# Chunked scan kernel: C sent compact and spread on chip, scores on row halves, loads and the first y reordered

## The chip, the cores and the metric

The kernel runs on one core of a Trainium2 chip. The metric is the device time of one execution in microseconds, the median of several runs; less is better.

## The reference

Three stages follow each other. The first is a chunked scan over 4 batches, 8 heads and 768 positions, head size 32, state size 16, chunks of 32 positions. The other two are a routed layer with 8 experts and a wide layer.

```python
for c in range(nc):                                    # 24 chunks
    cum = np.cumsum(la, axis=-1)
    L = np.exp(cum[..., :, None] - cum[..., None, :]) * causal
    M = np.einsum('bhin,bhjn->bhij', Cc, Bc) * L       # scores, masked
    y_intra = np.einsum('bhij,bhjd->bhid', M, xc)
    y_inter = np.einsum('bhin,bhnd->bhid', Cc, state) * np.exp(cum)[..., None]
    y[:, :, sl] = y_intra + y_inter
    state = decay_full * state + sum_j(Bc x xc * decay_from_j)
...
logits = x @ w_gate; e = argmax(logits); p = softmax(logits)[e]
out = p * (relu(x @ w1[e]) @ w2[e])
...
g = relu(x @ w_in) ** 2; return g @ w_out
```

## The kernel before, in words

The program is written out by hand for each engine: `manual_schedule` keeps the order in which the lines are called, and every engine, and every DMA queue, takes its instructions strictly in that order.

**Tiles and phases.** The scan (the function `attention`) works on 24 tiles of 128 tokens. Four tiles make a phase (a pair of batches, 256 positions), so there are six phases, 0 to 5; `ph, r = divmod(i, 4)` in the code. The loop `for i in range(-2, 24)` runs these steps, each a few tiles ahead of the next:

- `st_S` makes the scores. TensorE writes `sc` (C against B, L425), VectorE multiplies by the masked decay `Qm` into `M` (L428). It does so for tiles r = 0 and r = 1 of a phase, one batch each; r = 2 and 3 use the same `M`.
- `st_D` makes the state increments `dS` of two tiles on TensorE (L444), and `st_R` adds them on VectorE, 8 instructions a pair of tiles (L461). `dS` is one buffer for each batch, so the next `st_D` waits for the `st_R` before it.
- `st_Y` makes y on TensorE from `M` and X (L473) and from the state and C transposed, `CT` (L480). VectorE scales it into `row` (L485).
- `st_TT` transposes two tiles of rows on TensorE (`tp`, L502), and ScalarE copies them to `xt` (L505). `logits` (L511) and `logits2` (L518) turn four tiles of `xt` into gate logits.
- `gateA` picks the expert on VectorE; its first instruction is the maximum `mx` (L535). `gateB` counts ranks on TensorE (L557 to L561), VectorE makes slots from them (L566 to L571), and the queue stores the four rows to DRAM (`xs<-row`, L572). `spotA` makes one-hot tables, `lf` on VectorE (L581) and `lo` in five instructions on ScalarE (L591, L592). `spotB` multiplies them on TensorE (L602). `order` (L621 to L632) sorts the experts after phase 3.

The first `mx` of a phase's gate is a mark that comes four times in an even rhythm; the prediction measures stretches from mark to mark.

**Block layouts.** X for the increments and C for the scores lie in one tile `XC` ([128, 4, 2048], two buffers), each spread over four blocks with zeros between them: partition c, c+4, c+8, ... holds data only in block c. `blank_c` writes the zeros once (VectorE L315, ScalarE L312), and four loads a phase for X and four for C bring 32 partitions each (L290); in phases 0 to 2 some loads bring both halves. The C half is also doubled with zeros (`e`) on the host. So `sc` can be one matmul over 128 partitions for each head: 256 columns, 32 weight columns, four heads side by side in the four column strips of the array. `BB` holds B in two layouts (512 KB a phase, L284), `XA` is X for y, four loads a phase (L296), `CT` two loads (L300). `blank_x` zeroes XA, for the second buffer as two memsets on GpSimd (L662, L663).

**Queues.** All these loads go through SP's queue in the order of the calls. Eight semaphores are handed round among the DMAs, so a load waits until the eighth one before it has landed.

**The decay sums** `cum`, `cu2` borrow the score buffers (tag `sc`, two of one PSUM bank); `decay()` (L370, L371) writes into `cum` after the first increments.

After the scan come the routed layer (class `Moe`) and the wide layer (class `Mlp`), whose matmuls follow each other on TensorE.

## Time and profile before

| what | us |
|---|---|
| median of 3 runs | 511.07 (510.78 to 513.61) |
| the profiled execution's own time | 510.4 |
| its span, first to last instruction | 508.4 |
| TensorE busy | 491.3 (97%) |
| VectorE busy | 372.4 (73%) |
| ScalarE busy | 309.4 (61%) |
| GpSimd busy | 99.4 (20%) |
| bytes moved by DMA | 51.22 MB |

The profile gives one execution, with times from its first instruction. A row of the timeline says when a group of equal instructions started, how long it took in all, which line and tiles it has, and in brackets how long the engine had been idle before it and what ended that. TensorE's matmuls overlap, so the step from one start to the next tells more than the length of one. The scan fills roughly the first 80 us of the span.

### The profile page before, as it was taken

What the parts mean: (1) busy time and instruction counts of PE and PEld (TensorE: products, weight loads), DVE (VectorE), ACT (ScalarE), POOL (GpSimd) and SP (SyncE); (2) the same over time, 40 slices, a digit from 0 to 9 for tenths busy, and PEclk for the clock granted to TensorE, in tenths of its full rate; (3) what the DMA queues carried; (4) which work ended last, traced back from release to release, by engine and by line L of the source; (5) the groups of instructions that cost most, each with busy time, mean ns of one, the idle gap of its engine ahead of it and who ended that gap; (6) DMA issues with size and microseconds to landing.
All of it is one profiled execution on the core that took longest, in us unless ns stands there. A gap on an engine that the chain in (4) does not pass through costs nothing.

```text
span 508.4 us, 11650 instructions
## 1 busy us (share of the span) xinstructions
PE 491.3 (97%) x4537; PEld 459.1 (90%) x4537; DVE 372.4 (73%) x844; ACT 309.4 (61%) x636; POOL 99.4 (20%) x131
## 2 busy tenths in 40 slices
PE   7899798999999999999999999999999999999995
PEld 3677678899999999999999999899999999999995
DVE  8787688669898899994666767534888888676521
ACT  8332335376656666755986889776555555455684
POOL 6953210543331130000000000101500300031031
PEclk9999999999999999999999999999999999999999
DMA  8886866767676656530001100000100000010010
GB/s 258 271 254 219 276 196 209 227 163 191 188 222 169 176 193 191 183 84 2 2 1 43 43 0 1 12 10 12 74 2 0 23 23 1 1 43 1 1 43 24
DMA packets 20476, 51.22 MB, mean 101 GB/s; under 512 B 6561, under 2 KB 6690, under 8 KB 20418
## 3 DMA queue, kind: packets, MB, share of 16 engines
q1 hardware_dynamic: 17442, 43.04, 27.2%
q0 software_dynamic: 2832, 7.01, 5.1%
q8 instruction: 37, 0.61, 0.5%
q10 hardware_dynamic: 144, 0.40, 0.2%
q14 instruction: 21, 0.17, 0.1%
HBM read 44.06 MB, written 6.37 MB: 99 GB/s over the span
## 4 chain that ended last, share of the span: by engine, by line
PE 85%; issue 4%; ACT 3%; DVE 3%; DMA 2%; POOL 1%; SPq 1%; ACTq 0%; another core or an unknown queue 0%; POOLq 0%; DVEq 0%
PE u L1261 24%; PE o L953 14%; PE h L937 14%; PE h L1081 11%; PE h L1169 9%; PE u L1169 2%; DMA XC<-in_xc_dram 2%; PE dS L444 2%; PE y L473 2%; PE sc L425 2%; PE y L480 1%; PE tpm L918 1%; ACT XC L312 1%; PE tp L502 1%; DVE st L461 1%
## 5 line engine op out<-in xcount | busy, mean ns | idle before, releaser
L1261 PE MATMUL u<-wol,ga 128*128 128x256 f32 x384 | 108.0, 281 | 0.0
L1261 PE MATMUL u<-woh,ga 128*128 128x256 f32 x384 | 107.7, 281 | 0.0
L1261 PE MATMUL u<-woh,gb 128*128 128x256 f32 x384 | 107.7, 280 | 0.0
L1275 POOL DMA_INDIRECT out_dram<-ob,idx x24 | 26.6, 1109 | 278.9 <-ACT ob L1274 274.3
L1088 DVE TENSOR_TENSOR gb<-q,ga 128x256 fp32r<-128x256 f32 (+1 forms) x64 | 35.7, 558 | 57.5 <-ACT ga L1087 57.4
L1261 PEld LDWEIGHTS u<-woh,ga 128*128 128x128 f32 x384 | 72.3, 188 | 1.4
L1261 PEld LDWEIGHTS u<-wol,ga 128*128 128x128 f32 x384 | 72.3, 188 | 1.3
L1261 PEld LDWEIGHTS u<-woh,gb 128*128 128x128 f32 x384 | 72.5, 189 | 0.1
L940 ACT ACTIVATE hh<-h 128x256 fp32r<-128x256 f32 (+8 forms) x72 | 33.9, 472 | 52.6 <-PE h L937 49.0
L1081 PE MATMUL h<-zz,wih 128*128 128x512 f32 (+1 forms) x192 | 59.1, 356 | 0.0
L942 DVE SCALAR_TENSOR_TENSOR hl<-h,hh 128x256 fp32r<-128x256 f32 (+8 forms) x72 | 38.2, 530 | 16.9 <-ACT hh L940 16.8
L953 PE MATMUL o<-hl,whi 128*128 128x256 f32 (+8 forms) x144 | 47.6, 331 | 0.1
L953 PE MATMUL o<-hh,whi 128*128 128x256 f32 (+8 forms) x144 | 47.7, 331 | 0.0
L953 PE MATMUL o<-hh,wlo 128*128 128x256 f32 (+8 forms) x144 | 47.4, 329 | 0.2 <-DVE wlo L174 0.2
L937 PE MATMUL h<-xh,whi 128*128 128x208 f32 (+7 forms) x128 | 44.3, 346 | 0.2 <-DVE hl L942 0.2
L174 DVE TENSOR_TENSOR wlo<-wst,whi 128x512 fp32r<-128x512 f32 x64 | 43.2, 676 | 0.0
L937 PE MATMUL h<-xh,wlo 128*128 128x208 f32 (+7 forms) x128 | 42.9, 335 | 0.0
L937 PE MATMUL h<-xl,whi 128*128 128x208 f32 (+7 forms) x128 | 42.8, 335 | 0.0
L1085 ACT ACTIVATE q<-h 128x256 f32<-128x256 f32 (+1 forms) x64 | 30.9, 482 | 13.2 <-PE h L1081 11.3
L1081 PEld LDWEIGHTS h<-zz,wih 128*128 128x128 f32 x192 | 34.9, 188 | 4.3
L1169 PE MATMUL h<-zz,s 128*128 128x256 f32 x216 | 38.4, 286 | 0.0
L883 POOL DMA_INDIRECT xr<-xs,where x27 | 27.6, 1024 | 41.9 <-PE tpm L918 26.6
(250 smaller groups left out, 1191.6 us busy)
## 6 DMA issues: line engine op xcount, KB each, us to landing
wst<-in_wq_dram SPq DMA_DIRECT2D x32, 512.0 KB, 4.8
w<-in_win_dram SPq DMA_DIRECT2D x8, 512.0 KB, 6.5
w<-in_wout_dram SPq DMA_DIRECT2D x8, 512.0 KB, 4.3
XC<-in_xc_dram SPq DMA_DIRECT2D x28, 128.0 KB, 4.1
xs<-row SPq DMA_DIRECT2D x6, 516.0 KB, 4.0
BB<-in_bb_dram SPq DMA_DIRECT2D x6, 512.0 KB, 4.2
XA<-in_xa_dram SPq DMA_DIRECT2D x24, 128.0 KB, 3.8
XC<-in_xc_dram SPq DMA_DIRECT2D x10, 256.0 KB, 4.4
```

The lines of the kernel that those rows point to most:

```text
L174: eng.tensor_tensor(lo[:, w], st[:, w], hi[:, w].bitcast(F32), ALU.subtract)
L883: k.nc.gpsimd.indirect_dma_start(out=self.xr[key][:, j], out_offset=None, in_=rows, in_offset=bass.IndirectOffsetOnAxis(ap=at, axis=0))
L937: nc.tensor.matmul(ps, ring.up(wt, e, f, kd), xt[:, kd], start=(i == 0), stop=(i == 5))
L940: nc.scalar.activation(a, ps, ACTF.Relu)
L942: rest = lambda: nc.vector.scalar_tensor_tensor(b, ps, 0.0, a.bitcast(F32), ALU.max, ALU.subtract)
L953: nc.tensor.matmul(self.yps[e][d][:, c:c + n], ring.down(wt, e, f, d), ht, start=(f == 0 and i == 0), stop=(f == 7 and i == 2))
L1081: nc.tensor.matmul(ps, wt[:, kd, m * 128:m * 128 + 128], zt[t][:, kd], start=(i == 0), stop=(i == 5))
L1085: nc.scalar.activation(q, ps, ACTF.Relu)
L1088: nc.vector.tensor_tensor(b, q, a.bitcast(F32), ALU.subtract)
L1169: mm(o, w, z, start=start and i == 0, stop=True, skip_group_check=True)
L1261: nc.tensor.matmul(o, gt[:, q * 128:q * 128 + 128], wt[:, m], start=(m == first and i == 0 and h == 0), stop=(m == last and i == 2), skip_ ...
L1275: ins = nc.gpsimd.indirect_dma_start(out=k.out, out_offset=bass.IndirectOffsetOnAxis(ap=self.idx[:, c:c + 1], axis=0), in_=ob, in_offset=N ...
```

## The change

C is no longer sent with zeros. `bs` holds B and C side by side ([128, 1024], one load a phase, `load_s`), and the other layout of B is a load of its own (`bc`, 256 KB, `load_b`). Both have two buffers. `XC` shrinks to X alone ([128, 4, 1024]), and its four loads bring 128 KB each; the four loads of C are gone.

`expand(ph)` makes the spread C on chip, into `CB` (two buffers): four instructions of 128x512, each C times a column of zeros and ones (`C_POS`). For phase 0 VectorE does it, for the others ScalarE, in the loop at i = -1, 3, 7, 11 and 15, a phase ahead of its scores.

The scores of both batches of a phase are made at once at r = 0, into one `sc` of two banks. Each head is two matmuls instead of one, over partitions 0 to 63 and 64 to 127, of 128 columns each; the halves write different banks.

At the start, B and C are loaded ahead of X, CT goes behind X, and the blanks are shared out anew: ScalarE's of XC 0 go to VectorE, and each is half as long. `fills()` moves from VectorE's start to GpSimd after phase 2's preparation (i = 3). The first y (`st_Y(0)`) moves ahead of the second increments, and the first M ahead of the last two state updates. `cum` and `cu2` are the halves of `sc`; `decay()` writes to `small`.

```diff
-    cc = np.zeros((NPH, 4, 2, NS, 2, 2, 256), np.float32)
-    for e in range(2):
-        cc[:, :, e, :, :, e] = cr[:, :, e]
...
-    bs = turn4(br.transpose(3, 0, 4, 6, 1, 2, 5).reshape(NPH, 128, 2, 256))
+    br, cr = (z.reshape(2, 2, NH, NG, 8, 32, NS).transpose(3, 0, 4, 6, 1, 2, 5).reshape(NPH, 128, 512) for z in (B, C))
+    bs = np.concatenate([br, cr], 2)
...
-    ps_s = body.enter_context(tc.tile_pool(name="ps_s", bufs=2, space=bass.MemoryType.PSUM))
+    ps_s = body.enter_context(tc.tile_pool(name="ps_s", bufs=1, space=bass.MemoryType.PSUM))
...
+    def load_s(ph):
+        sp.dma_start(out=BS[ph % 2], in_=k.bs[ph])
+    def expand(ph):
+        for q in range(4):
+            o, c, pos = CB[ph % 2][:, q], BS[ph % 2][:, 512:1024], cst[:, C_POS + q:C_POS + q + 1]
+            if ph:
+                s.activation(o, c, ACTF.Copy, scale=pos)
+            else:
+                v.tensor_scalar(o, c, pos, None, ALU.mult)
...
-        for hq in range(2):
-            for h4 in range(4):
-                h = hq * 4 + h4
-                pe.matmul(sc[32 * h4:32 * h4 + 32, hq].rearrange("p (c e) f -> p c e f", e=2), BB[ph % 3][:, 0, b2, h * 32:h * 32 + 32],
-                          Cb[p][:, :, b2, :, h * 32:h * 32 + 32], start=(hq == 0), stop=True, skip_group_check=True)
+        for bb in (0, 1) if r == 0 else ():
+            for hq in range(2):
+                for rr in range(2):
+                    half = slice(64 * rr, 64 * rr + 64)
+                    for h4 in range(4):
+                        h = hq * 4 + h4
+                        o = bb * 256 + hq * 128
+                        pe.matmul(sc[32 * h4:32 * h4 + 32, rr, o:o + 128].rearrange("p (q f) -> p q f", q=4),
+                                  BS[p][half, bb * 256 + h * 32:bb * 256 + h * 32 + 32],
+                                  Cb[p][half, :, bb, h * 32:h * 32 + 32], start=(hq == 0), stop=True, skip_group_check=True)
...
     prep(0, (0,))
-    fills()
...
         if i == -2:
-            st_R(0, (0, 1, 2, 3))
+            st_R(0, (0, 1, 2))
         stage(st_S, i + 2)
+        if i == -2:
+            st_R(0, (3,))
+        if i == 3:
+            fills()
+        if i == 0:
+            st_Y(0)
...
         if i % 4 == 3 and 2 < nx < NPH:
             load_b(nx)
-            load_c(nx, XS)
+        if i >= -1 and i % 4 == 3 and nx < NPH:
+            load_s(nx)
+        if i % 4 == 3 and 0 < (i + 5) // 4 < NPH:
+            expand((i + 5) // 4)
...
-            load_c(i // 4 + 2, XT if i else slice(0, 2))
+            load_c(i // 4 + 2)
```

**Where it moves instructions.** ScalarE, from the zeroing of the second CT to the first gate (CB is the spread C, BS the load that holds C, xt the copied transposed rows, ls the copied logits). Before:

```order
L312 ACTIVATE CT_124<-zt 64x512 x2
L505 ACTIVATE xt<-tp 128x512
L312 ACTIVATE CT_125<-zt 64x512 x2
L505 ACTIVATE xt<-tp 128x512
L514 ACTIVATE ls<-small 128x128
```

and now:

```order
L317 ACTIVATE CT_127<-zt 64x512 x2
L294 ACTIVATE CB_121<-BS_123,cst 128x512 x4
L514 ACTIVATE xt<-tp 128x512
L317 ACTIVATE CT_128<-zt 64x512 x2
L294 ACTIVATE CB_120<-BS_122,cst 128x512 x4
L514 ACTIVATE xt<-tp 128x512
L523 ACTIVATE ls<-small 128x128
```

The spread for phase 2 stands ahead of the second copy to xt, on which the first logits wait.

ScalarE again, in phase 4 as it now stands (lo of the third spot table, the spread for phase 5, the copy of the rows of tiles 14 and 15, ls of phase 3):

```order
L600 ACTIVATE lo<-cst,lf 128x128 x4
L601 ACTIVATE lo<-lo 128x512
L294 ACTIVATE CB_121<-BS_123,cst 128x512 x4
L514 ACTIVATE xt<-tp 128x512
L523 ACTIVATE ls<-small 128x128
```

Here too the spread stands directly ahead of a copy to xt. At i = 7 and 11 it stands behind the copy of one pair of tiles and ahead of that of the next.

SP's queue, from the loads of phase 1's B to those of phase 2's X, with waits (a DMAHW name is one of the eight semaphores; BS_0 is phase 2's). Now:

```order
L281 DMA BC_1_125<-in_bc_dram 128x512 [waits DMAHW6_49]
L284 DMA BS_1_123<-in_bs_dram 128x1024 [waits DMAHW7_49]
L288 DMA XC_1_117<-in_xc_dram 32x1024 [waits DMAHW0_49,DVE_49]
...
L301 DMA XA_1_119<-in_xa_dram 32x1024 [waits DMAHW6_49,Pool_49]
L301 DMA XA_1_119<-in_xa_dram 32x1024 [waits DMAHW7_49]
L305 DMA CT_1_127<-in_ct_dram 64x512 [waits DMAHW0_49]
L305 DMA CT_1_127<-in_ct_dram 64x512 [waits DMAHW1_49]
L281 DMA BC_0_124<-in_bc_dram 128x512 [waits DMAHW2_49]
L284 DMA BS_0_122<-in_bs_dram 128x1024 [waits DMAHW3_49,PE_49]
L288 DMA XC_0_116<-in_xc_dram 32x1024 [waits DMAHW4_49,PE_49]
```

Phase 2's C now comes in BS_0, behind XA, whose second pair of loads waits for GpSimd's memset, and behind CT; before, it came with XC at the place of the last row.

## Rows read from the trace of the kernel before

**Rows 1.** The page: busy time of the engines.
```profile
PE 491.3 (97%) x4537; PEld 459.1 (90%) x4537; DVE 372.4 (73%) x844; ACT 309.4 (61%) x636; POOL 99.4 (20%) x131
```
**Rows 2.** Windows: busy time of each engine, clock, DMA share, GB/s.
```profile
40.00:60.00 20.00, 17.25 (x452) 13.56 (x445) 16.09 (x64) 6.25 (x19) 7.37 (x16) 1.00 0.75 237
100.00:120.00 20.00, 20.00 (x134) 18.65 (x134) 14.47 (x32) 15.05 (x29) 9.88 (x10) 1.00 0.61 144
```
**Rows 3.** Chain of waits, its two DMA pieces: start us, us, what.
```profile
22.64 5.12 DMA XC<-in_xc_dram
...
47.97 3.83 DMA XC<-in_xc_dram
```
**Rows 4.** VectorE's timeline: the four gate marks and the stalls between them.
```profile
27.76 0.18 DVE L535 TENSOR_REDUCE mx<-small 128x4 f32<-128x32 f32 x1
...
39.30 0.18 DVE L535 TENSOR_REDUCE mx<-small 128x4 f32<-128x32 f32 x1
...
49.65 0.76 DVE L485 TENSOR_TENSOR row<-y,Pd 128x256 f32<-128x256 f32 x2 [1.86 <-DMA xs<-row]
...
50.42 0.18 DVE L535 TENSOR_REDUCE mx<-small 128x4 f32<-128x32 f32 x1
...
62.43 0.19 DVE L535 TENSOR_REDUCE mx<-small 128x4 f32<-128x32 f32 x1 [1.11 <-PE small L518]
```
**Rows 5.** SP's queue: phase 1's CT, the store of phase 0's rows.
```profile
17.81 1.16 SPq L300 DMA_DIRECT2D CT<-in_ct_dram  x2
...
45.44 0.52 SPq L572 DMA_DIRECT2D xs<-row  x1
```
**Rows 6.** TensorE's timeline: logits of phase 0, phase 2's transposes, then phase 3.
```profile
25.86 0.62 PE L511 MATMUL small<-xt,cst 128*32 128x128 f32 x16
...
34.90 0.66 PE L502 MATMUL tp<-cst,row 128*128 128x128 f32 x4
...
39.02 1.07 PE L425 MATMUL sc<-XC,BB 128*32 128x256 f32 x16
39.90 1.06 PE L444 MATMUL dS<-XC,Bt 128*32 128x128 f32 x32
40.89 0.66 PE L502 MATMUL tp<-cst,row 128*128 128x128 f32 x4
...
42.38 1.05 PE L425 MATMUL sc<-XC,BB 128*32 128x256 f32 x16
43.24 0.62 PE L473 MATMUL y<-XA,M 128*32 128x128 f32 x16
...
45.48 0.66 PE L502 MATMUL tp<-cst,row 128*128 128x128 f32 x4
```
**Rows 7.** VectorE's timeline in phase 3, between the second and third mark.
```profile
40.39 0.67 DVE L428 TENSOR_TENSOR M<-sc,Qm 128x512 f32<-128x512 f32 x1
40.97 2.15 DVE L461 SCALAR_TENSOR_TENSOR st<-st,Gm,dS 128x128 f32<-128x128 f32 x8
43.04 0.42 DVE L485 TENSOR_TENSOR row<-y,Pd 128x256 f32<-128x256 f32 x1
...
44.71 0.18 DVE L566 TENSOR_TENSOR ix<-small,hot 128x32 f32<-128x32 f32 x1
...
45.35 0.16 DVE L581 SCALAR_TENSOR_TENSOR lf<-lh,slots 128x4 f32<-128x4 int32 x1
```
**Rows 8.** ScalarE's timeline: lo of the first table, the copy to xt in phase 4.
```profile
36.08 1.27 ACT L591 ACTIVATE lo<-cst,lf 128x128 fp32r<-128x128 f32 x4
37.38 0.63 ACT L592 ACTIVATE lo<-lo 128x512 fp32r<-128x512 f32 x1
...
60.41 0.60 ACT L505 ACTIVATE xt<-tp 128x512 f32<-128x512 f32 x1 [2.31 <-PE tp L502]
```
**Rows 9.** GpSimd's timeline: the second memset of XA.
```profile
14.93 1.81 POOL L663 MEMSET XA<- 128x2048 f32 x1
```
**Rows 10.** The tile BB: from issue to landing of its six 512 KB loads.
```profile
DMA to landing us min/median/max: 3.7/4.2/4.9
```

## The prediction

> **What bounds the kernel now.** I read the page first. TensorE is busy for 491 of the 508 us [rows 1], so only a stretch in which it is not full can give anything without removing matmuls. The windows show where: from 40 to 60 us TensorE counts 17.25 of 20 us, and from 100 us on 20.00 of 20, at clock 1.00 both times [rows 2]. All that the change touches lies in the scan, in the first 80 us; a us won there moves the full part forward as a whole, since its loads are issued in step with its own work. In the scan nothing is full: VectorE has 16.09 of 20 us, ScalarE 6.25 and the DMA engines 0.75 [rows 2]. So the chain of waits is next. It passes over X and C twice: a load that takes 5.12 us ahead of phase 2's scores, and one of 3.83 us ahead of phase 4's increments [rows 3]. VectorE's timeline says the same from another side: the store of phase 0's rows holds it for 1.86 us [rows 4], because the store stands in SP's queue until 45.44 [rows 5]. SP is late: each load waits for the eighth before it to land, and a phase has 16 transfers.

> I measure by four marks, the maxima that begin a gate [rows 4]: 27.76, 39.30, 50.42 and 62.43. The stretches are A to the first mark, B 11.54, C 11.12, D 12.01, and E, all behind.

> **The change part by part.**

> *Fewer loads.* A phase falls from 16 transfers to 13 (four of C go, one for the second layout of B comes) and by 256 KB. Five phases have 15 transfers less between them, so the load waits of the chain and the store's stall should go from phase 2 on. What is late next is whatever stands on VectorE, TensorE and ScalarE without waits; that is worked out below for B and C.

> *Scores on halves.* Scores of one batch step on after 0.88 and 0.86 us [rows 6]; two a phase make 1.74. Half as many columns, twice as many matmuls: if the row halves run side by side as the four column strips already do, both batches take 0.87; if they do not, 1.74 stays, and a gain over the half has no reason. No row here has row halves. I take 0.87, since 16 matmul records of four strips in 0.88 us with 1.07 us from first to last end already show strips side by side. [...]
> Against the change: the step from increments to scores within one strip shape is 0.86 to 0.88, that from increments to transposes, where the array changes from strips to whole, 0.99 [rows 6]. So a change of shape costs some 0.12, and the scores now bring one more a phase; 0.1 is in the terms below. [...]

> *B and C.* Without waits, TensorE goes from scores to the second transposes in 45.48 - 39.02 = 6.46 less the second scores' 0.86, plus 0.1: 5.7 [rows 6]. Scores start 0.28 before the mark, so the transposes stand at 5.4. VectorE is there in time: gate 1.09, M 0.58, eight updates 2.07, then two rows and an M, some 1.4, are 5.1 [rows 4, 7]. From those transposes to the mark it took 34.90 to 39.30, 4.40 [rows 4, 6]; this goes over ScalarE's copy and lo. The new stretch is 9.8. B gives 11.54 - 9.8 = **-1.7**, C 11.12 - 9.8 = **-1.3**. If the halves do not overlap, 0.87 of each is not there. The spread in these phases lies between two copies to xt, with 3 us of room, and is hidden; the fills on GpSimd lie in its idle time ahead of the second mark and cost nothing.

> *The spread on ScalarE.* No row has it. The nearest is the 128x512 instruction of 0.63 us [rows 8]; four are 2.5. Below it cannot fall much, as the copy to xt of the same size takes 0.60. Above: L591 has an operand for each partition as the spread has, and four of 128 columns take 1.27, so the operand costs at most some 0.3 each, and the spread at most 3.7. I take 2.5, by the size.

> *A.* The spread for phase 2 waits for its load and holds the copy on which phase 0's logits wait. The load stands behind GpSimd's second memset, which ends at 16.74 [rows 9], two loads of XA and the two of CT, done at 18.97 [rows 5]; then comes the small load of B, some 0.6 as one of CT. So it is issued at 19.6, and lands after 3.7 to 4.9, median 4.2 [rows 10]: 23.8. With 2.5 for the spread and 0.6 for the copy, less overlaps, the logits start at 26.8, and from there to the mark it took 27.76 - 25.86 = 1.90 [rows 4, 6]: 28.7 against 27.76, **+1.0**. What the start gains (fewer blanks on ScalarE, M and y earlier, by my reading half a us) ends in this wait. Were the wait not there, A would give -0.5.

> *D.* VectorE needs 1.09, 0.58, 2.07, a row of 0.35 and 0.80 from ix to the end of lf [rows 7]: 4.9. Then lo 1.9 [rows 8] makes 6.8, and now the spread for phase 5 stands there: 9.3. From the copy's start to the mark it took 62.43 - 60.41 = 2.02 [rows 4, 8], so the mark comes after 11.4: 12.01 - 11.4 = **-0.6**. Without the spread in between it would be 8.8, -3.2.

> *E* keeps its length, **0**: the sort of the experts on VectorE holds the next increments there, so half the scores' time was hidden.

> The sum is +1.0 - 1.7 - 1.3 - 0.6 = -2.6. The profiled execution has 510.4 and would have 507.8; the median shown is 0.7 higher, 511.07, and becomes **508.4**. A measurement of this kernel can tell about 0.5%, 2.6 us, so this lies on the edge, at 508.5.

> **The rivals.**
> *The spreads are not in the way* (phase 2's C lands early, or ScalarE's order costs less than I think). For it: ScalarE is idle 2.31 us ahead of the copy in phase 4 [rows 8]. Against it: both spreads stand directly ahead of a copy that is waited for. With A -0.5 and D -3.2 the sum is -6.7: 504.4; with one of the two, some 506.
> *The row halves run one after the other.* Then B and C lose 0.87 each: -0.9, 510.2. For it: no row shows halves side by side.
> *The change does not do what it says*: the loads were late by bandwidth, not by count, and with 0.75 of the DMA engines busy the next load takes the place of the one removed; the stall of 1.86 stays. Then only B gives something, against A: 510.5 to 511.5.
> *Slower:* the spread on ScalarE is long. At 1.0 us for each instruction it takes 4.0, which adds 1.5 in A and D and, beyond the room of 3 us, 1.0 in B and in C: +5.0. With a landing after 4.9 instead of 4.2 it is +5.7, and the sum +3.1: 514.2. It decides from 0.95 an instruction on, where the sum passes +2.6. Against it: L592's 0.63. [...]

> **How the numbers follow.** Forecast 0.45, its own range from the landing (3.7 to 4.9) and the spread (2.4 to 3.0) some 507.5 to 509.8; spreads out of the way 0.27; halves in a row 0.11; bandwidth 0.10; slower 0.07. The range reaches from the middle of the first rival's ground, 505.0, to 511.3, past the halves and most of the bandwidth case. Faster by over 0.5% (below 508.5): 0.27 and a little over half of the forecast, 0.51. Slower by over 0.5% (above 513.6): 0.07. The rest, 0.42, is within.

> **What would show it.** The marks: near 28.7, 38.5, 48.3 and 59.7. The first falls behind 27.76 if the spread holds the logits; ScalarE's copy before it then starts right at the end of the spread, and the spread at a landing. Scores of a phase, 32 program matmuls, should step on after 0.9 us; 1.7 shows the halves in a row. The store of phase 0's rows should be issued near 36, and no row of VectorE wait for it. In phase 4 lo, spread and copy should follow each other on ScalarE without a gap. The forecast is wrong if the first mark comes before 27.5 or the fourth's stretch is under 10.

## The result, and the profile after

The changed kernel takes 513.89 us (median of 22 executions) against 511.1 of the kernel before (22 executions beside them): a ratio of 1.006, with a 95% interval of 1.0039 to 1.0080. It is slower by 0.6%, outside the range given. Here and below, ratios and clocks leave out executions over 1.5% above the fastest of the same kernel (two of a_fewer, one of a_third).

The profiled execution of the changed kernel has a span of 513.7 us against 508.4 of before. Its own time is 515.5, 1.6 above the median, and that of before lay 0.7 below its own; so of the 5.3 us between the two profiles some 2.3 are the luck of these two executions. The page of the changed kernel, its engines, TensorE's clock and the queue of instructions:

```profile
PE 491.4 (96%) x4729; PEld 461.4 (90%) x4729; DVE 372.9 (73%) x841; ACT 317.8 (62%) x655; POOL 100.2 (20%) x139
...
PEclk9999997999999999999999999999999999999998
...
q8 instruction: 39, 0.64, 0.5%
```

TensorE is busy as long as before (491.3, [rows 1]), with 192 matmul records more. The clock line has a 7 in the seventh slice, which the kernel before has not. VectorE's timeline of the changed kernel, the marks up to the fourth (the same rows as in [rows 4]):

```profile
30.27 0.43 DVE L494 TENSOR_TENSOR row<-y,Pd 128x256 f32<-128x256 f32 x1 [2.34 <-PE y L489]
30.61 0.18 DVE L544 TENSOR_REDUCE mx<-small 128x4 f32<-128x32 f32 x1
...
42.41 0.18 DVE L544 TENSOR_REDUCE mx<-small 128x4 f32<-128x32 f32 x1
...
50.79 0.99 DVE L494 TENSOR_TENSOR row<-y,Pd 128x256 f32<-128x256 f32 x2
...
52.72 0.18 DVE L544 TENSOR_REDUCE mx<-small 128x4 f32<-128x32 f32 x1
...
64.70 0.19 DVE L544 TENSOR_REDUCE mx<-small 128x4 f32<-128x32 f32 x1 [2.92 <-PE small L527]
```

| stretch | before | forecast | after |
|---|---|---|---|
| A, to the first mark | 27.76 | 28.7 | 30.61 |
| B | 11.54 | 9.8 | 11.80 |
| C | 11.12 | 9.8 | 10.31 |
| D | 12.01 | 11.4 | 11.98 |
| E in the scan, fourth to last mark | 18.39 | 18.4 | 18.51 |
| last mark to the end | 427.6 | 427.6 | 430.5 |

The changes of the six rows are +2.85, +0.26, -0.81, -0.03, +0.12 and +2.9: 5.3. Half lies at the start of the scan, half behind it. The rows of VectorE at 50.79 no longer wait for a store, as they did at 49.65 [rows 4]. What they and the marks wait for stands in TensorE's timeline of the changed kernel:

```profile
15.96 0.41 PE L482 MATMUL y<-XA,M 128*32 128x128 f32 x7
17.72 0.52 PE L482 MATMUL y<-XA,M 128*32 128x128 f32 x9 [1.34 <-issue]
...
20.20 1.16 PE L431 MATMUL sc<-CB,BS 64*32 64x128 f32 x64
21.29 1.44 PE L453 MATMUL dS<-XC,Bt 128*32 128x128 f32 x32
24.57 1.08 PE L453 MATMUL dS<-XC,Bt 128*32 128x128 f32 x32 [1.84 <-DVE st L470]
...
27.85 0.52 PE L520 MATMUL small<-xt,cst 128*32 128x128 f32 x10 [0.40 <-ACT xt L514]
...
29.37 0.31 PE L482 MATMUL y<-XA,M 128*32 128x128 f32 x3 [0.67 <-issue]
...
34.88 0.52 PE L482 MATMUL y<-XA,M 128*32 128x128 f32 x10 [1.37 <-issue]
...
53.49 0.84 PE L431 MATMUL sc<-CB,BS 64*32 64x128 f32 x36 [0.40 <-issue]
...
58.50 0.53 PE L489 MATMUL y<-st,CT 128*32 128x128 f32 x12 [0.65 <-issue]
...
63.33 0.63 PE L520 MATMUL small<-xt,cst 128*32 128x128 f32 x12 [1.16 <-ACT xt L514]
```

"issue" means that the engine waited for nothing the profile shows. Five times TensorE stops so, in the middle of a row of equal matmuls, for 4.43 us in all; in the profile of before it does so once, for 0.33:

```profile
29.95 0.43 PE L444 MATMUL dS<-XC,Bt 128*32 128x128 f32 x8 [0.33 <-issue]
```

Counting TensorE's records (matmuls, weight loads and the semaphore instructions between them) from the start, 449, 961, 1217, 2241 and 2497 of them stand ahead of the five stops: they differ by multiples of 256. The one stop of before also has 961 ahead of it, at another line of the program. The page has 39 packets of 16 KB on the instruction queue, and TensorE's 9529 records are some 37 times 256; in before they are 37 packets and 9152 records, some 36 times 256. From these counts I estimate that a packet stands for 256 records, and read a stop as the records of one packet used up before the next packet is there; what a packet holds is not shown. I call them **stops at the border**. The times of the packets agree with this (below, a_light). The line of the page of before:

```profile
q8 instruction: 37, 0.61, 0.5%
```

Windows of the changed kernel behind the scan (columns as in [rows 2]):

```profile
80.00:84.00 4.00, 3.11 (x29) 3.02 (x28) 3.83 (x13) 1.83 (x7) 0.40 (x1) 1.00 1.00 301
84.00:91.00 7.00, 6.63 (x37) 6.47 (x36) 4.45 (x17) 2.61 (x5) 0.00 (x0) 0.51 0.51 183
91.00:95.00 4.00, 3.89 (x33) 3.68 (x32) 2.75 (x8) 1.85 (x4) 1.06 (x2) 1.00 0.52 167
```

The first two windows in the kernel before, at the same distance from its last mark:

```profile
77.60:81.60 4.00, 3.11 (x29) 3.02 (x28) 3.83 (x13) 1.83 (x7) 0.40 (x1) 1.00 0.95 310
81.60:88.60 7.00, 6.19 (x54) 5.81 (x53) 5.52 (x23) 4.23 (x8) 0.00 (x0) 1.00 0.61 198
```

From 84 to 91 us the granted clock is 0.51 (in windows of 1 us it is 1.00 from 60 to 84, 0.50 from 85 to 90 and 1.00 again from 91 to 100; I call 0.50 the lower level), behind a stretch with an idle 0.89 us; the kernel before has the same 0.89 idle there, and no fall behind it, so this wait alone does not make the fall. 37 matmuls pass where the kernel before has 54 at 1.00. At some 0.12 us from one to the next (6.19 us busy for the 54) the 17 are by estimate 2.0 us, most of the 2.9 behind the scan; at 122.6 us a wait of 1.12 us for a load of the routed layer follows, which the kernel before has not.

### The profile page after: what moved, and what is told of

The parts are those of the page before. It is cut to its first block, busy times and chain, and to the rows that moved or that the text cites. A ratio compares the mean times of both kernels' runs of the same rounds, so it can differ in the third digit from the quotient of the medians.

```text
span 513.7 us, 12041 instructions
## 1 busy us (share of the span) xinstructions
PE 491.4 (96%) x4729; PEld 461.4 (90%) x4729; DVE 372.9 (73%) x841; ACT 317.8 (62%) x655; POOL 100.2 (20%) x139
## 4 chain that ended last, share of the span: by engine, by line
PE 79%; DMA 6%; issue 5%; ACT 4%; DVE 3%; POOL 2%; POOLq 0%; another core or an unknown queue 0%; DVEq 0%; ACTq 0%
PE u L1279 23%; PE h L955 12%; PE o L971 12%; PE h L1099 11%; PE h L1187 9%; PE u L1187 2%; DMA xr<-xs,where 2%; PE dS L453 2%; PE y L482 1%; DMA mc<-xr 1%; PE sc L431 1%; POOL xr L901 1%; PE y L489 1%; DMA XC<-in_xc_dram 1%; DMA BS<-in_bs_dram 1%
## 5 line engine op out<-in xcount | busy, mean ns | idle before, releaser
L971 PE MATMUL o<-hh,whi 128*128 128x256 f32 (+8 forms) x144 | 48.3, 335 | 0.0
L1103 ACT ACTIVATE q<-h 128x256 f32<-128x256 f32 (+1 forms) x64 | 30.9, 483 | 13.1 <-PE h L1099 11.3
L901 POOL DMA_INDIRECT xr<-xs,where x27 | 29.0, 1073 | 38.6 <-PE tpm L936 20.9
```

Source lines behind the costliest of these rows:

```text
L901: k.nc.gpsimd.indirect_dma_start(out=self.xr[key][:, j], out_offset=None, in_=rows, in_offset=bass.IndirectOffsetOnAxis(ap=at, axis=0))
L971: nc.tensor.matmul(self.yps[e][d][:, c:c + n], ring.down(wt, e, f, d), ht, start=(f == 0 and i == 0), stop=(f == 7 and i == 2))
L1103: nc.scalar.activation(q, ps, ACTF.Relu)
```

## The experiments

Sixteen runs were made in five groups: eleven edited kernels, and five runs that repeat a kernel. Each group ran on one chip beside executions of the kernel before, so a ratio compares within the group; absolute times differ between groups (before had medians of 510.5 to 515.5). The table has for each: four marks and the last one of the scan, the stops at the border of 0.25 us or more up to the last mark, the time from 11 us to the last mark in which TensorE had neither matmul, weight load nor semaphore instruction, the median over the executions of the mean granted clock, and the ratio to before. Marks, stops and idle time are those of one profiled execution.

| kernel | marks 1 to 4, last | stops | idle | clock | ratio (95%) |
|---|---|---|---|---|---|
| before | 27.76 39.30 50.42 62.43 80.82 | 0.33 | 5.0 | 0.998 (one) | 1 |
| changed | 30.61 42.41 52.72 64.70 83.21 | 4.43 | 11.8 | 0.991 | 1.006 (1.0039 to 1.0080) |
| b_again | 28.29 39.78 50.54 62.52 82.29 | 1.01 | 5.4 | 0.9935 | 1.0006 (0.9972 to 1.0039) |
| a_again | 30.88 42.41 53.62 65.19 86.26 | 3.65 | 11.0 | 0.988 | 1.0103 (1.0046 to 1.0160) |
| a_third | 30.34 42.13 52.17 65.28 85.73 | 4.21 | 11.8 | 0.990 | 1.0072 (1.0035 to 1.0108) |
| b_split | 31.41 42.94 53.63 64.03 83.86 | 2.80 | 7.9 | 0.9915 | 1.0040 (1.0003 to 1.0078) |
| a_fewer | 29.78 39.93 51.59 62.96 83.81 | 1.73 | 9.2 | 0.9885 | 1.0018 (0.9992 to 1.0043) |
| a_light | 29.21 39.42 50.70 61.94 81.51 | 0.80 | 8.3 | 0.991 (one) | one execution |
| a_light2 | 29.29 40.69 51.28 62.67 81.99 | 1.36 | 8.9 | 0.991 | 0.9999 (0.9976 to 1.0023) |
| a_late | 30.28 41.34 54.45 66.73 86.66 | 2.62 | 13.7 | 0.988 | 1.0122 (1.0094 to 1.0150) |
| a_fill | 30.43 45.10 55.12 66.42 87.73 | 5.26 | 14.9 | 0.985 | 1.0145 (1.0081 to 1.0209) |
| a_whole | 29.19 46.18 56.76 67.98 87.84 | 0 | 10.5 | 0.989 | 1.0111 (1.0062 to 1.0160) |
| a_whole2 | 30.46 41.77 53.43 63.19 82.88 | 0 | 9.2 | 0.997 | 1.0037 (1.0017 to 1.0056) |
| b_order | 28.45 39.58 51.88 61.55 80.04 | 0.27 | 4.8 | 0.997 | 0.9982 (0.9964 to 1.0000) |
| b_order2 | 28.51 39.94 51.30 63.31 83.18 | 0 | 6.2 | 0.995 | 1.0014 (0.9979 to 1.0048) |
| b_short | 27.35 39.62 49.80 60.84 78.79 | 0.28 | 7.4 | 0.995 | 0.9997 (0.9973 to 1.0022) |
| b_rows | 27.77 42.38 52.95 62.72 81.06 | 0 | 6.3 | 0.996 | 0.9994 (0.9974 to 1.0015) |
| bo_rows | 27.91 39.77 50.45 62.17 80.67 | 1.01 | 5.8 | 0.994 | 1.0021 (0.9997 to 1.0044) |

**Both kernels again** (b_again, a_again, a_third), without an edit.

> The kernel before, unchanged. Two theories of what the change lost: (1) TensorE stops at the borders of its instruction stream (every 256 records), 4.4 us in all in the changed kernel's profile, 0.33 us in that of before; (2) behind the scan TensorE's clock falls to 0.50 for 6.8 us, which before's profile does not have. If both belong to the change, this run shows under 1 us of such stops and a mean clock of 0.998 in most of its executions. If either is chance, stops or clocks of 0.991 turn up here as well.

> The changed kernel, unchanged. If stops and fall of the clock belong to it: stops of 3 to 5 us in all at borders 256 records apart, a mean clock of 0.988 to 0.994, and a ratio of 1.004 to 1.008 to before. If they were chance: stops under 1 us, clock 0.998, and a time near 508 to 509 us.

> The changed kernel, unchanged, beside the others on one chip. Both theories: ratio 1.006 to 1.012, stops of 3 to 5 us, mean clock 0.985 to 0.992, idle of TensorE from 11 us to the last mark 10 to 13 us.

Stops, first mark and idle time repeat: 3.6 to 4.4 us of stops in three profiles of the changed kernel, 0.3 and 1.0 in two of before. The clock does not divide them so cleanly. The kernel before is lower in some executions too (b_again's 12 have mean clocks of 0.987 to 1.000, with a median of 0.9935, not 0.998), and beside the kernel before (medians of 0.993 and 0.996) the changed one stands 0.005 and 0.006 lower. So "clock 0.998 for before" was a miss. Nor does the fall have one place: in the profiles (their last few us left out, where all fall) it lies at 84 us in the changed kernel, at 31, 65 and 106 us in a_again, at 63 and 104 us in a_third, and at 100 us in b_again, which is the kernel before. By these means the changed kernel loses more time at the lower level; falls as such are not its own.

**b_split**: the kernel before with twice as many score instructions and nothing else.

```diff
-                pe.matmul(sc[32 * h4:32 * h4 + 32, hq]..., Cb[p][:, :, b2, :, ...], start=(hq == 0), ...)
+                for x in range(2):
+                    pe.matmul(sc[32 * h4:32 * h4 + 32, hq, 4 * x:4 * x + 4]..., Cb[p][:, 2 * x:2 * x + 2, b2, :, ...],
+                              start=(hq == 0 and x == 0), ...)
```

> The kernel before, with each matmul of the scores cut into two of 128 columns: as many columns, twice as many instructions for the scores, as in the change, and nothing else of it. Theory stops: TensorE's stops at borders 256 records apart grow from 0.3 to 1.5 us or more, and the time by 1 to 3 us. Rival, that the stops come from the loads or from the order of the change: stops under 1 us, time within 0.5 us of before. Scores should still take 0.9 us a batch.

TensorE's timeline of b_split, its scores in phase 1 and the stop:

```profile
19.94 1.11 PE L426 MATMUL sc<-XC,BB 128*32 128x128 f32 x32
...
30.17 0.30 PE L475 MATMUL y<-XA,M 128*32 128x128 f32 x2 [2.80 <-issue]
```

The scores take no longer themselves; the stop at record 961 grows from 0.33 and 0.64 to 2.80 us, and the first mark moves from 28.29 (b_again) to 31.41. The time rises by 0.4%, with an interval from nothing to 0.8%. A first mark three us late is had from the number of instructions alone, without the spread, the new loads or the new order.

**a_fewer**: half the instructions of the changed kernel's scores left out from phase 1 on.

```diff
-                for rr in range(2):
+                for rr in (0, 1) if ph == 0 else (0,):
```

> The changed kernel with the second row half of the scores left out from phase 1 on (its output is not the reference's): 128 records of TensorE less in each phase, as many for the scores as in the kernel before; everything else is as in the change. Theory number: stops of the first three marks fall from 3.5 us to under 1.5, the last mark of the scan comes 2 to 4 us earlier than the changed kernel's 83 to 86. Rival, traffic alone: stops of 2 us or more in all, marks within 1 us.

The stop at 961 is gone; those left are 1.73 us in all, the forecast of under 1.5 ahead of the third mark is just missed, and B is 10.15 instead of 11.80. The last mark, "2 to 4 us earlier" by the forecast, is 2.45 and 1.92 earlier than in a_again and a_third (86.26, 85.73), and 0.60 later than in the first profile (83.21). The row of its scores also settles another point:

```profile
29.55 1.08 PE L431 MATMUL sc<-CB,BS 64*32 64x128 f32 x32
30.56 1.08 PE L453 MATMUL dS<-XC,Bt 128*32 128x128 f32 x32
```

One row half alone steps on after 1.01 us, both halves together (20.20 to 21.29 above) after 1.09. The halves run side by side.

**a_light, a_light2**: the changed kernel with a quarter of X.

```diff
-            sp.dma_start(out=XC[ph % 2][c:128:4, c], in_=k.xc[ph, c:128:4])
+            sp.dma_start(out=XC[ph % 2][c:32:4, c], in_=k.xc[ph, c:32:4])
...
-            at = slice(32 * c, 32 * c + 32)
+            at = slice(32 * c, 32 * c + 8)
```

> The changed kernel, but each load of X (both layouts) brings a quarter of its rows, so every second term of the sums is left out and the output is not the reference's; the instructions, their number and their waits are the same, and a phase moves 1.25 MB instead of 2. Theory traffic: TensorE's stops at the borders of 256 records are blocks of instructions that come late behind the loads, so they shrink from 2.3 us ahead of the first mark to under 0.5, and the first mark comes at 28.5 us or earlier. Rival, that the number of instructions alone makes them: stops of 2 us ahead of the first mark as before, mark at 30.5.

> The changed kernel with light loads of X once more, in several executions. If the falls of the clock follow from the stops, its mean clock is at 0.994 or above and its time 0.990 to 0.997 of before; if they follow from the other waits of the change, the clock stays at 0.986 to 0.992 and the time at 0.997 to 1.002.

With the same instructions and fewer bytes the stops shrink from 4.43 to 0.80 and 1.36, and ahead of the first mark there is none in either. So number and traffic both matter: fewer instructions (a_fewer, 1.73 us left) or fewer bytes (a_light, 0.80) took most of the stops away, and twice the score instructions beside the old loads (b_split) brought one of 2.80 back. The trace also holds the times of the packets on the instruction queue, and they show the link. The third packet belongs to the border at 961, in us:

| kernel | TensorE passes 705 | third packet | TensorE passes 961 | stop |
|---|---|---|---|---|
| before | 24.17 | 27.32 to 28.44 | 29.95 | 0.33 |
| changed | 21.65 | 26.84 to 28.06 | 29.37 | 0.67 |
| b_split | 21.72 | 27.50 to 28.67 | 30.17 | 2.80 |
| a_light | 20.26 | 22.47 to 23.47 | 27.96 | none |

In all 18 profiles each stop of the table ends 1.2 to 1.7 us behind the end of its border's packet, and none of the first twelve borders is passed less than 1.17 us behind it. In the sixteen profiles with all the loads the third packet starts at 26.3 to 27.9 us, however early TensorE is; with light loads it starts some 4 us sooner. The mark follows because of where its work stands: the transposed logits (`logits2`) begin at record 876 in the kernel before and 939 in a_fewer, ahead of the border, but at 1003 in the changed kernel and 1004 in b_split, behind it. In the three profiles of the changed kernel and in b_split the first mark comes 1.24 to 1.25 us behind the passing of 961. Why the packet is late (the loads ahead of it, or what else they hold up) is not taken apart further.

The first mark came at 29.21 and 29.29, later than the 28.5 expected, and the clock stayed at 0.991: the rival in a_light2's expectation. TensorE's timeline and the windows of a_light2 show where it falls:

```profile
23.27 1.08 PE L453 MATMUL dS<-XC,Bt 128*32 128x128 f32 x32 [1.85 <-DVE st L470]
...
61.15 0.63 PE L520 MATMUL small<-xt,cst 128*32 128x128 f32 x12 [1.90 <-ACT xt L514]
```

```profile
20.00:24.00 4.00, 2.15 (x89) 1.71 (x79) 3.46 (x11) 0.50 (x2) 4.00 (x9) 1.00 0.83 255
24.00:28.00 4.00, 4.00 (x75) 3.22 (x68) 2.64 (x9) 2.63 (x5) 3.73 (x16) 0.57 0.76 207
58.00:62.00 4.00, 1.88 (x24) 1.13 (x21) 1.21 (x5) 3.27 (x7) 0.00 (x0) 1.00 0.02 6
62.00:66.00 4.00, 3.84 (x103) 2.99 (x103) 2.50 (x15) 0.78 (x5) 0.00 (x0) 0.58 0.29 113
79.00:82.00 3.00, 2.24 (x21) 2.15 (x20) 2.93 (x9) 1.34 (x3) 0.37 (x1) 1.00 0.99 289
82.00:89.00 7.00, 6.50 (x35) 6.34 (x36) 4.48 (x21) 3.08 (x7) 0.03 (x1) 0.53 0.51 175
```

Each fall (0.57, 0.58 and 0.53 in these windows) stands right behind a stretch in which TensorE waits: for VectorE's updates (1.85 us, 1.04 in the profile of before), for the copy that stands behind the spread (1.90), for the routed layer's first weights (0.89, as long in before). The waits do not decide alone: the changed kernel's profile has the first of them too (1.84 us at 24.57 above) and no fall behind it. The first two belong to the change: scores of both batches in 1.09 us bring TensorE to the increments sooner, where VectorE is not ready, and the spread for phase 5 holds the copy.

**a_fill**: matmuls without use in TensorE's last two idle stretches.

```diff
+        if i == 20:
+            keep(14)
         if i >= 0:
             stage(st_D, i + 2)
...
     gateA(5, 20, 4)
+    keep(14)
```

> The changed kernel with 14 matmuls of 128 columns ahead of the last increments and 14 ahead of the routed layer's first matmul, in TensorE's two last idle stretches of the scan (1.00 and 0.89 us); their results are not used. Theory clock: the clock stays at 1.00 behind the scan, the mean is 0.998, and the time falls by 2 to 3 us against the changed kernel. Rival, that the clock falls for what lies earlier (idle at 62 to 66 us) or without a cause in TensorE's work: clock 0.991, time as the changed kernel or 0.2 us more.

Clock and time are the worst of the table, but the edit did not fill the gaps. TensorE's timeline of a_fill, the added matmuls (L649):

```profile
75.99 0.94 PE L649 MATMUL sc<-ones 128*128 128x128 bf16 x14 [2.72 <-DVE M L436]
87.86 1.55 PE L649 MATMUL sc<-ones 128*128 128x128 bf16 x14 [0.89 <-DVE wlo L948]
```

They write into `sc`: the first fourteen wait until VectorE has read it for M, so the idle stretch of 1.00 became one of 2.72, and the other fourteen start behind the 0.89 us, not in it. The clock falls from 36.8 us, behind a stop of 2.74, and again at 88 and 108. So this run says nothing of the theory; whether filling the gaps would keep the clock up is open.

**a_late**: the spreads behind the copy.

```diff
-        if i % 4 == 3 and 0 < (i + 5) // 4 < NPH:
-            expand((i + 5) // 4)
+        if i == -1:
+            expand(1)
...
             logits(i // 4 - 1)
+            expand(i // 4 + 1)
```

> The changed kernel with the spreads for phases 2 to 5 called a tile later, behind the copy to xt and the first logits. Theory queue: the spread holds the copy for some 0.4 us ahead of the first mark and 1.2 us ahead of the fourth, so A falls by 0.4 and the stretch from third to fourth mark by 1.5 to 3 us (to 9 to 10.4), the time by 1 to 3 us. Rival, that the stops or the increments set those marks anyway: the stretches within 0.5 us of the changed kernel's 11.3 to 12.0.

A falls by 0.33 only: its first mark too stands 1.24 us behind the passing of the border at 961 (29.04, with a stop of 1.00 there). In phase 4 the copy no longer stands behind the spread. But the scores of phases 3 and 4 now wait for the spread, as TensorE's timeline of a_late shows:

```profile
42.72 1.63 PE L431 MATMUL sc<-CB,BS 64*32 64x128 f32 x64 [1.59 <-ACT CB L294]
...
55.82 1.21 PE L431 MATMUL sc<-CB,BS 64*32 64x128 f32 x64 [1.59 <-ACT CB L294]
```

Neither theory was right: the wait moved, C grew to 13.11, and D came at 12.28, not at 9 to 10.4.

**b_order, b_order2, b_rows, bo_rows**: only the order of the change in the kernel before; then a fourth buffer for the rows, without and with it.

```diff
-    load_t(0)
...
-    load_c(0, XT, (0, 1))
-    load_c(0, cs=(2, 3))
-    load_c(0, XS, (0, 1))
+    load_c(0)
+    load_t(0)
...
-            st_R(0, (0, 1, 2, 3))
+            st_R(0, (0, 1, 2))
         stage(st_S, i + 2)
+        if i == -2:
+            st_R(0, (3,))
+        if i == 3:
+            fills()
+        if i == 0:
+            st_Y(0)
```

```diff
-    rowp = ctx.enter_context(tc.tile_pool(name="arow", bufs=3))
+    rowp = ctx.enter_context(tc.tile_pool(name="arow", bufs=4))
```

> The kernel before with only the order of the change: CT loaded behind XC, X and C of phase 0 in four loads, the fills on GpSimd at i = 3, first y ahead of the second increments, first M ahead of the last two updates. Compact C, the spread and the row halves stay out. Theory: what the change lost comes from the halves' instructions, so the first mark comes at 27.3 to 28.3 us and the time within 1.5 us of before, faster if at all. Rival, that the order itself delays the start: first mark at 29.5 or later, slower by 1 to 3 us.

> The reordered kernel before once more: 0.9982 with an interval of 0.9964 to 1.0000 at its first run. If the order gives something, the ratio comes out at 0.996 to 0.999 again; if that was chance, 0.999 to 1.002.

> The kernel before with four row buffers in place of three, so that phase 3's rows no longer wait for the store of phase 0's. Theory: VectorE's waits of 1.86 and 1.90 us on the store go; the third and fourth mark come 1 to 3 us earlier, and the time falls by 0.5 to 2 us. Rival, that the loads behind the same backlog (XC for the increments, 3.83 us in the chain) take the place: marks within 0.5 us, time as before.

> The reordered kernel before with four row buffers. The reordered one waited 2.98 and 1.45 us on the store. Theory: both go, the stretch from second to third mark falls from 12.3 to about 10.5 us, and the time to 0.992 to 0.996 of before. Rival, as for four buffers alone: no more than the reordered kernel's 0.998.

The order costs nothing (first mark 28.45 and 28.51) and gives nothing that repeats: 0.9982, then 1.0014. The wait for the store, which the prediction read as a loss of the kernel before, goes with four buffers, and the time stays (0.9994, 1.0021): the rival of both expectations in the time, though not in b_rows' marks. Its second mark comes 3.1 us late, as TensorE's timeline of b_rows shows, and the stretches C and D behind it are together 2.8 us shorter:

```profile
30.02 1.93 PE L425 MATMUL sc<-XC,BB 128*32 128x256 f32 x16 [2.39 <-DMA BB<-in_bb_dram]
```

In this profile a load of the same queue took the place of the store. The wait on the store was not worth its length.

**b_short**: less work for TensorE, no more instructions.

```diff
+                w = 4 if ph else 8
-                pe.matmul(sc[32 * h4:32 * h4 + 32, hq]..., Cb[p][:, :, b2, :, ...], ...)
+                pe.matmul(sc[32 * h4:32 * h4 + 32, hq, 0:w]..., Cb[p][:, 0:w // 2, b2, :, ...], ...)
```

> The kernel before with the scores of phases 1 to 5 made for half the columns only (M takes them twice, so the output is not the reference's): as many instructions, loads and waits, but TensorE has 0.4 us a batch less to do in the scan, as the row halves make it. Theory: a TensorE with less to do between its waits falls to clock 0.50 more often, so the median of the mean clock falls from about 0.995 to 0.990 or lower although no stop at the instruction borders is added (under 1 us), and the time does not fall, or rises by up to 2 us. Rival, that the falls of the changed kernel come from its stops: clock as before within 0.002, time 0 to 2 us shorter.

The clock stays with that of before (0.995; the executions of before beside it 0.997) and so does the time. Less work by itself did not lower the clock by more than these 0.002 here, and scores shorter by some 0.4 us a batch (by estimate, half of the 0.88 of before) did not shorten the run by a measurable amount either, although the last mark of its profile is the earliest of all.

**a_whole, a_whole2**: compact C, but scores on whole rows, so that TensorE has as many score instructions as before. C is spread over eight blocks.

```diff
-        for bb in (0, 1) if r == 0 else ():
...
-                for rr in range(2):
-                    half = slice(64 * rr, 64 * rr + 64)
...
+                pe.matmul(sc[32 * h4:32 * h4 + 32, b2, hq * 256:hq * 256 + 256].rearrange("p (q f) -> p q f", q=8),
+                          BS[p][:, b2 * 256 + h * 32:b2 * 256 + h * 32 + 32], Cb[p][:, :, b2, h * 32:h * 32 + 32], ...)
...
-        for q in range(4):
+        for q in qs:
...
+            if ph > 1 and q > 3:
+                g.tensor_scalar(o, c, pos, None, ALU.mult)
```

> The changed kernel with the scores on whole rows again: C is spread over eight blocks (ScalarE four and GpSimd four instructions a phase; eight on ScalarE for phase 1, four each on VectorE and ScalarE for phase 0), one matmul of 256 columns for each head, one batch at a time. The loads and the rest are as in the change; TensorE has as many score instructions as before. Theory number: the loss is that of the halves, so stops ahead of the first mark fall from 2.3 us to under 1, TensorE's idle time from 11 us to the last mark from 11 to 15 us to under 8, the mean clock stands at 0.993 or above, and the time at 0.996 to 1.003 of before. Rival, that compact C (the spread, its landing and the queue of ScalarE) costs it: ratio 1.006 or more, first mark at 29.5 or later with few stops.

> The whole-row kernel with the spread shared out anew: GpSimd took 1.55 us for each instruction, and the scores of phase 2 waited 3.91 us for it, so in phase 2 it does two, VectorE two and ScalarE four; in phase 5 ScalarE's four stand behind the copy to xt. Theory: without the halves there are no stops at the instruction borders, and without that wait the second mark comes 10 to 11 us after the first, the last one at 81 to 84 us, with TensorE idle for less than 7 us, clock 0.993 or above, time 0.995 to 1.002 of before. Rival, that compact C costs the start whatever spreads it: ratio 1.005 or more, first mark at 29.5 or later.

In both profiles no stop at a border is left. The first form put a wait of its own in: TensorE's and GpSimd's timelines of a_whole.

```profile
32.97 1.93 PE L430 MATMUL sc<-CB,BS 128*32 128x256 f32 x16 [3.91 <-POOL CB L294]
```

```profile
26.73 6.19 POOL L294 TENSOR_SCALAR CB<-BS,cst 128x512 f32<-128x512 f32 x4
```

The second form has no such wait on GpSimd and a clock of 0.997 (before beside it 0.994), and is still slower than before by 0.37%: between its theory (up to 1.002) and its rival (1.005 or more), whose late first mark came. B, 11.31, and the idle time of 9.2 us are longer than the theory had them. ScalarE's and TensorE's timelines of a_whole2 show what holds the first mark at 30.46: the load of phase 2's C ends ScalarE's wait at 25.48, and the spread stands ahead of the copy.

```profile
25.48 2.56 ACT L296 ACTIVATE CB<-BS,cst 128x512 f32<-128x512 f32 x4 [3.55 <-DMA BS<-in_bs_dram]
27.94 0.57 ACT L511 ACTIVATE xt<-tp 128x512 f32<-128x512 f32 x1
```

```profile
28.57 0.52 PE L517 MATMUL small<-xt,cst 128*32 128x128 f32 x10 [1.50 <-ACT xt L511]
```

So compact C costs in A without the halves too (here with more spreads than in the change, eight for phase 1), and the halves bring the stops on top. No kernel here beats the one before by a margin that repeats.

## Why the prediction was wrong, step by step

**Fewer loads**: right in direction, with a wrong count. The loads of X, B and C are 36 instead of 44 over the six phases: three fewer in each of phases 3 to 5, but one more in phases 1 and 2, whose loads of XC brought both halves before; "15 transfers less" does not hold. SP is less backlogged later on, the store of phase 0's rows is issued at 39.98 instead of 45.44 [rows 5] (36 was forecast), no row of VectorE waits for it, and no load of X or C holds TensorE in phases 2 to 4. That this would pay was wrong: with four row buffers in the kernel before the wait goes too, and the time stays.

**Scores on halves, the time of the matmuls**: right. 1.09 us for both batches against 0.87 and 0.1 forecast, and a_fewer shows the halves side by side. The rival of halves in a row falls. The rows that the prediction read as a step from increments to scores go from scores to increments and from scores to y [rows 6]; b_split has the step that it meant (20.81 to 21.69), 0.88 as well.

**Scores on halves, "twice as many matmuls": here the prediction failed.** The sum priced the columns and the change of shape and gave the instructions nothing. TensorE's stops at the border took 2.01 us ahead of the first mark, 1.37 in B and 1.05 in D. Taken off, the stretches would be 28.60, 10.43, 10.31 and 10.93 against the forecast 28.7, 9.8, 9.8 and 11.4; from the first mark's +0.84 to D the sum is -2.2, where -2.6 was forecast. Taking off is an estimate and an upper bound, since a stop can hide another wait: of the 2.01 only the 0.67 at 961 surely stands on the way to the mark (see A), and with it alone the sum is -0.8. b_split and a_fewer say the same from two sides, by adding such instructions alone and by leaving them out. The profile of before had a trace of it: one stop of 0.33 us with "issue" as its reason, which the prediction left unpriced.

**The spread on ScalarE**: right in size and place. Four instructions took 2.56 and 2.54 us (2.5 forecast), the load of phase 2's C landed at 24.67 (23.8 forecast; the row names VectorE's update, which ended at the same time, while a_third's names the load, at 24.66), and the copies follow the spreads without a gap:

```profile
24.76 2.56 ACT L294 ACTIVATE CB<-BS,cst 128x512 f32<-128x512 f32 x4 [3.71 <-DVE st L470]
27.22 0.58 ACT L514 ACTIVATE xt<-tp 128x512 f32<-128x512 f32 x1
...
60.25 2.54 ACT L294 ACTIVATE CB<-BS,cst 128x512 f32<-128x512 f32 x4
62.70 0.57 ACT L514 ACTIVATE xt<-tp 128x512 f32<-128x512 f32 x1
```

**A measured by its mark** was +2.85 for +1.0. On the path that the prediction drew, the logits behind the copy start at 27.85 where it had 26.8, which is +1.05, most of it from the landing (24.67 against 23.8); from there to the mark it takes 2.76 instead of 1.90, and 0.67 of that is the stop at 961. So the landing was mis-sized and the stop was missing. Which of the two is longer changes from profile to profile: in a_again the landing comes at 23.6 and the logits at 26.79, as forecast, and the stop is 1.99. In a_whole2, without stops, the landing at 25.4 alone holds the mark back. Whether the first stop, 1.34 us at 17.7, delays that load is not shown.

**D**: its path (lo, spread, copy, logits) is as forecast, with lo 0.7 later. The parts given add up to 11.3, not 11.4; this changes nothing.

**"E, 0", and "a us won there moves the full part forward as a whole"**: the scan's part of E kept its length (+0.12), but the part behind it did not. I took clock 1.00 for granted behind the scan, because one profile of before had it. Both kernels have executions with a lower mean clock (down to 0.984 in before and 0.981 in the changed kernel, in a_again's group), and the changed kernel has more of this: beside each other its median clock is 0.988 against 0.993, and 0.990 against 0.996. In the 29 executions of before in b_short's group, time and clock go together at 3.4 us for each 0.01 (3.3 to 4.0 in three other groups, 1.0 in a_fewer's), so 0.006 is, by estimate, about 2 us of the changed kernel's loss. In a_light2 three falls (0.57, 0.58 and 0.53) stand behind waits of 1.85, 1.90 and 0.89 us; that curing the waits would cure them is not shown. b_short (0.995 beside 0.997) speaks against less work as the cause, a_fewer (0.9885 with stops of 1.73 us) and a_light2 (0.991 with 1.36) against the stops as the only one; a_whole2 has neither halves nor stops, and a clock no lower than that of before (0.997 beside 0.994). The cause of the falls stays open.

**The rivals.** The slower one (a long spread) had the right sign and the wrong mechanism: 0.64 us an instruction, where it needed 0.95. Bandwidth falls with the store's earlier issue, though traffic came back in another place, in the stops. "Spreads not in the way" falls with a_late: moved away from the copies, they hold the scores. The two signs by which the prediction would have known itself wrong, a first mark before 27.5 and a fourth stretch under 10, both looked for a kernel that gains too much; neither came.

## What to carry to other kernels

Count the instructions that an edit adds to the engine that bounds the kernel, and look in the profile of before for stops with "issue" as their reason: here the one of 0.33 us stood at record 961, where b_split, with twice the score instructions, stopped for 2.80 us and a_light, with fewer bytes, not at all (the DMA engines' share in before is 0.91 from 24 to 34 us). Whether a mark's work stood ahead of that record or behind it decided how late the mark came: in the changed kernel and b_split, where it stood behind, the mark followed the passing of 961 by 1.24 to 1.25 us. A wait that an engine off the bound removes is worth nothing until it is shown to be on the path; a cheap experiment with one more buffer tells (b_rows: the wait gone, the time 0.9994). Idle time on TensorE may cost twice, once as it passes and once in a slower stretch behind it: waits of 1.85, 1.90 and 0.89 us in a_light2 had windows at a granted clock of 0.57, 0.58 and 0.53 behind them, though one of 1.84 us in the changed kernel had none. So a split that makes TensorE faster in short bursts and then lets it wait can, by this estimate, lose.
